# Attention with pooled keys and a routed MLP on one core: even blocks of batches 0 to 2 turn one key tile on TensorE instead of two

## The chip, the core and the metric

The kernel runs on one core of one Trainium2 chip. The metric is the device time of one execution in microseconds (us); lower is better. A comparison takes the kernel before and the changed kernel in turn on the same chip.

## The reference

For each of four batches there are 12288 queries of 128 channels and a key/value map that is pooled 4x4 to 768 rows and multiplied with `w_sr`; keys and values are the same rows. The attention output then goes through a routed MLP: the 128 rows with the highest gate score are replaced by themselves plus a gated two-layer MLP.

```python
def _attn_ref(q, kv, w_sr):
    kv_pool = kv.reshape(B, H // r, r, W // r, r, C).mean(axis=(2, 4))   # r = 4
    k = v = kv_pool.reshape(B, -1, C) @ w_sr
    s = (q @ k.transpose(0, 2, 1)) / np.sqrt(C)
    a = np.exp(s - s.max(-1, keepdims=True))
    a /= a.sum(-1, keepdims=True) + 1e-09
    return a @ v

def _moe_ref(x, w_gate, w1, w2, capacity):
    scores = np.einsum('bsd,d->bs', x, w_gate)
    for b in range(B):
        top = np.argpartition(-scores[b], capacity)[:capacity]
        ye = np.maximum(x[b, top] @ w1, 0.0) @ w2
        out[b, top] = x[b, top] + sigmoid(scores[b, top])[:, None] * ye
```

## The kernel before

The queries are cut into 192 blocks of 256 (48 a batch). A block has two query tiles of 128, so 2 x 768 = 1536 score columns, that is 12 key tiles of 128x128. One main loop runs over the blocks, `for i in range(nb)`, and its body writes out by hand the order in which each engine gets its instructions; every instruction is chained to the one before it on its engine (`InOrder`, line 54), so nothing is reordered later. All instructions therefore have line 54 in the profile, and one goes by the names of the tiles.

In iteration i: TensorE forms the scores of block i+1 in PSUM (`S`, tile `s`, two buffers of three banks, each score as three matmuls: `kl,qh`, `kb,ql`, `kh,qh`) and multiplies the turned exponentials of block i-5 with the values (`AV`, tile `o_two`, 36 matmuls). VectorE takes the row maxima of block i (`s_max`, tile `m`). ScalarE takes the exponentials of block i (`exp`, tile `am`). These have to be turned (transposed) before they can be multiplied with the values, as an f16 high half and a bf16 low half (`hl` before turning, `at` after it). There are two ways:

- Most tiles go through the DMA queue: `to_high` (a cast on ScalarE) and `to_low` (a subtraction on GpSimd) write the two halves into `hl`, and `turn` issues one DMA transposition for each half from SyncE. `hl` has four buffers, `at` six.
- The last `turned(n)` tiles of the block are turned by TensorE (`turn_pe`, matmul `s<-cst,am`), into the PSUM bank that the exponentials have left free. ScalarE then casts them and VectorE subtracts, straight into `at`.

Where fewer than two tiles are turned by TensorE, `own(n)` is 256: ScalarE leaves 256 columns of exponentials in PSUM (`exp` part 1 in place), casts them from there (`hl<-s`), and VectorE takes their low halves in the next iteration instead of GpSimd. `main(n)` is the number of columns that is left for GpSimd; DMA turns `main(n) + own(n)`. Before the change, blocks of batches 0 to 2 have two tiles turned, own 0 and main 1280, so DMA turns 10 tiles in each half. In batch 3 even blocks have none turned, own 256 and main 1280 (12 tiles by DMA), odd blocks one turned, own 256 and main 1152 (11 tiles).

SyncE issues all plain loads and stores and all transpositions from one queue: in each pair of blocks four transpositions, one load of q (256 KB), one store of the output (256 KB), and, while a batch's successor is prepared (`next_keys`, batches 0 to 2), quarter loads of kv (256 KB). GpSimd also adds up the kv rows for the pooling (`kv_sum`) and takes the low halves of the queries (`ql`, every second block). Every few blocks TensorE projects a pooled key tile, and from the second batch on a selection of the 128 rows of the batch before (`topk`, `pick`) runs beside the blocks.

Of the kernel before, what the change touches and what calls it, by code (L numbers as in the profile page):

```python
# [30 lines left out]
NBLK = N // BLK  # L31
# [37 lines left out]
def attention_topk_mlp(ctx, tc, a, outs, capacity):  # L69
# [343 lines left out]
    def direct(n):  # L413
        return n >= nb - 2

    def turned(n):
        return 2 if n < 3 * NBLK else 0 if direct(n) else n % 2

    def own(n):
        return OWN if turned(n) < 2 and not direct(n) else 0  # L420

    def main(n):
        return 2 * M - turned(n) * P - own(n)
# [25 lines left out]
    def turn_pe(n):  # L449
        st[n]["bank2"] = []  # L450
        for c in range(turned(n)):
            lo = 2 * M - (turned(n) - c) * P
            r = pe.transpose(s_flat[n % 2][:, lo:lo + P], st[n]["a"][:, main(n) + c * P:main(n) + (c + 1) * P], ident)
            others(r, [st[n]["exp1"]])
            st[n]["bank2"].append(r.ins)
# [436 lines left out]
    n = nb - 1  # L892
# [154 lines left out]
```

## Time and profile before

| | |
|---|---|
| median of 3 runs | 930.14 us (926.39 to 936.0) |
| profiled execution | 928.83 us, its span 927.1 us |
| TensorE (PE) busy | 891.5 us, 96% |
| ScalarE (ACT) busy | 756.4 us, 82% |
| GpSimd (POOL) busy | 737.7 us, 80% |
| VectorE (DVE) busy | 700.3 us, 76% |
| mean granted TensorE clock | 0.991 |
| DMA moved | 209.82 MB, mean 226 GB/s |

The engines' shares are means over the whole span. Matmuls are pipelined, so a matmul's own duration overlaps that of its neighbours; the pace of TensorE is read from the distance between the starts of things that happen once in a block. A DMA share is the time that packets took, over 16 engines; packets overlap, so it can exceed 1. SPq is the issuing queue of SyncE.

### The profile page before, as it was taken

The page shows a single profiled execution, that of the slowest core. Times are in us where ns is not written, and L with a number is a line of the kernel's source. Part 1 is how long each engine was busy: PE and PEld are TensorE (multiplying, and loading weights), DVE is VectorE, ACT ScalarE, POOL GpSimd, SP SyncE. Part 2 cuts the span into 40 slices and gives each one's busy share as a digit, 9 for nine tenths or more (in the row PEclk, how much of TensorE's full clock was granted, in tenths as well). Part 3 has the DMA queues.
Part 4 walks back from the last instruction along what each step waited for, and adds up shares of the span by engine and source line. Part 5 has one row for each costly group of instructions (what it writes and reads, how often), then busy time and mean ns, then how long its engine had stood idle before and what let it go on. Part 6 is the DMA issues. An engine that isn't in the chain of part 4 may idle for free.

```text
span 927.1 us, 26215 instructions
## 1 busy us (share of the span) xinstructions
PE 891.5 (96%) x10151; PEld 722.3 (78%) x10151; DVE 700.3 (76%) x1861; ACT 756.4 (82%) x1238; POOL 737.7 (80%) x511
## 2 busy tenths in 40 slices
PE   4899999999999999999999999999999999999966
PEld 4678887887788878787787888887788787878865
DVE  6667666767678877777767887888767888888874
ACT  2788888888988888888988888888898988898841
POOL 2788988998898989888888898898787777777711
PEclk9999999999999999999999999999999999999978
DMA  9999999999999999999999999999999999999960
GB/s 363 204 197 237 237 235 244 227 236 245 205 228 236 225 238 235 235 237 217 235 242 230 234 239 229 237 240 219 232 225 225 240 241 231 231 243 231 221 126 21
DMA packets 563517, 209.82 MB, mean 226 GB/s; under 512 B 527040, under 2 KB 528576, under 8 KB 563008
## 3 DMA queue, kind: packets, MB, share of 16 engines
q1 hardware_dynamic: 563136, 207.62, 111.1%
q8 instruction: 79, 1.29, 0.6%
q0 software_dynamic: 256, 0.52, 0.2%
q14 instruction: 46, 0.38, 0.1%
HBM read 52.04 MB, written 25.43 MB: 84 GB/s over the span
## 4 chain that ended last, share of the span: by engine, by line
PE 76%; POOL 9%; issue 6%; DMA 4%; DVE 3%; ACT 2%; SPq 0%; POOLq 0%; DVEq 0%; ACTq 0%
PE s L54 41%; PE o_two L54 34%; POOL hl L54 3%; POOL kv_sum L54 3%; DMA at<-hl 3%; POOL ql L54 2%; DMA kv_raw<-in_kv 1%; ACT am L54 1%; DVE junk L54 1%; PE lot L54 1%; ACT hl L54 0%; DVE m L54 0%; DMA xe<-out,idx 0%; SPq L54 0%; DVE pooled L54 0%
## 5 line engine op out<-in xcount | busy, mean ns | idle before, releaser
L54 POOL TENSOR_TENSOR hl<-am,hl 128x1280 bf16<-128x1280 f32 x192 | 499.3, 2600 | 130.9 <-ACT hl L54 65.0
L54 PEld LDWEIGHTS <-at 128*128 128x128 f16 (+1 forms) x6912 | 399.7, 97 | 54.3 <-issue 51.4
L54 PE MATMUL o_two<-vx,at 128*128 128x130 f16 x6768 | 430.3, 220 | 2.6 <-POOL vx L54 1.5
L54 ACT ACTIVATE am<-s,m 128x512 f32<-128x512 f32 (+1 forms) x528 | 358.3, 706 | 37.6 <-DVE m L54 26.5
L54 DVE TENSOR_REDUCE m<-s 128x2 f32<-128x1536 f32 x191 | 335.5, 1757 | 48.8 <-PE s L54 48.8
L54 PE MATMUL s<-kh,qh 128*128 128x256 f32 (+1 forms) x771 | 362.3, 472 | 0.0
L54 PE MATMUL s<-kl,qh 128*128 128x256 bf16 (+1 forms) x771 | 255.2, 331 | 1.1 <-DVE pm L54 0.9
L54 PE MATMUL s<-kb,ql 128*128 128x256 bf16 (+1 forms) x771 | 250.5, 325 | 1.7 <-POOL ql L54 0.6
L54 ACT CAST hl<-am 128x1280 f16<-128x1280 f32 x192 | 240.4, 1252 | 8.6 <-DMA at<-hl 2.7
L54 PEld LDWEIGHTS s<-kh,qh 128*128 128x128 f32 x771 | 146.3, 190 | 47.6
L54 DVE TENSOR_TENSOR at<-s,at 128x256 bf16<-128x256 f32 (+1 forms) x167 | 67.7, 406 | 91.7 <-ACT at L54 91.7
L54 POOL TENSOR_TENSOR ql<-q_raw,qh 128x512 bf16<-128x512 f32 x96 | 122.5, 1276 | 11.7 <-ACT qh L54 11.7
L54 PEld LDWEIGHTS <-qh 128*128 128x128 bf16 x771 | 75.0, 97 | 58.6 <-issue 49.2
L54 ACT CAST at<-s 128x256 f16<-128x256 f32 (+1 forms) x167 | 59.7, 357 | 67.5 <-PE s L54 67.4
L54 PEld LDWEIGHTS <-ql 128*128 128x128 bf16 x771 | 76.1, 99 | 8.9 <-POOL ql L54 5.7
L54 DVE TENSOR_TENSOR x<-o_two,rz 128x256 f32<-128x256 f32 x186 | 77.4, 416 | 0.0
L54 DVE TENSOR_SCALAR rz<-o_two,sg 128x2 f32<-128x2 f32 x187 | 40.6, 217 | 33.4 <-PE o_two L54 32.5
L54 PE MATMUL s<-cst,am 128*128 128x128 f32 x311 | 62.1, 275 | 2.2 <-ACT am L54 2.1
L54 ACT CAST qh<-q_raw 128x512 fp32r<-128x512 f32 x96 | 59.5, 619 | 3.8 <-DMA q_raw<-in_q 3.8
L54 POOL TENSOR_TENSOR kv_sum<-kv_raw 128x256 f32<-128x256 f32 x72 | 52.7, 732 | 0.0
L54 PEld LDWEIGHTS s<-cst,am 128*128 128x128 f32 x311 | 36.4, 140 | 4.8 <-ACT am L54 3.8
L54 DVE RECIPROCAL rz<-rz 128x2 f32<-128x2 f32 x190 | 31.6, 166 | 6.5
(209 smaller groups left out, 545.5 us busy)
## 6 DMA issues: line engine op xcount, KB each, us to landing
out<-x SPq DMA_DIRECT2D x94, 256.0 KB, 4.1
q_raw<-in_q SPq DMA_DIRECT2D x93, 256.0 KB, 3.3
kv_raw<-in_kv SPq DMA_DIRECT2D x70, 256.0 KB, 4.1
at<-hl SPq DMA_TRANSPOSE x384, 4.1
kv_raw<-in_kv SPq DMA_DIRECT2D x3, 1024.0 KB
kv_raw<-in_kv SPq DMA_DIRECT2D x5, 512.0 KB, 10.2
q_raw<-in_kv SPq DMA_DIRECT2D x2, 512.0 KB
w<-in_w SPq DMA_DIRECT2D x2, 512.0 KB, 8.3
```

Source lines behind the costliest of these rows:

```text
L54: r = f(*args, **kwargs)
```

## The change

`turned(n)` gives 1 in even and 2 in odd blocks of batches 0 to 2, where it gave 2 in all. `own` and `main` follow from it by the unchanged lines under it: even blocks then have own 256 and main 1152.

```diff
     def turned(n):
-        return 2 if n < 3 * NBLK else 0 if direct(n) else n % 2
+        return 1 + n % 2 if n < 3 * NBLK else 0 if direct(n) else n % 2
 
     def own(n):
         return OWN if turned(n) < 2 and not direct(n) else 0
 
     def main(n):
         return 2 * M - turned(n) * P - own(n)
```

TensorE, in an even block of batch 0, the difference (s_113 and s_114 are the two score buffers, `cst` holds the identity):

```order
 L54 MATMUL s_114<-kh,qh 128x256
 L54 MATMUL s_113<-cst,am 128x128 [waits Activation_49]
-L54 MATMUL s_113<-cst,am 128x128
 L54 LDWEIGHTS qh
 L54 MATMUL s_114<-kl,qh 128x256
```

One of the two turning matmuls is gone; nothing else moves on TensorE there.

SyncE, a stretch of batch 1, before:

```order
L54 DMA out<-x 128x512
L54 DMA_TRANSPOSE at<-hl 128x10x128 x2
L54 DMA q_raw<-in_q 128x512
L54 DMA_TRANSPOSE at<-hl 128x10x128
L54 DMA kv_raw<-in_kv 128x512
L54 DMA_TRANSPOSE at<-hl 128x10x128
L54 DMA out<-x 128x512
```

and the same stretch after the change:

```order
L54 DMA out<-x 128x512
L54 DMA_TRANSPOSE at<-hl 128x11x128 x2
L54 DMA q_raw<-in_q 128x512
L54 DMA_TRANSPOSE at<-hl 128x10x128
L54 DMA kv_raw<-in_kv 128x512
L54 DMA_TRANSPOSE at<-hl 128x10x128
L54 DMA out<-x 128x512
```

The order is the same; both transpositions of an even block carry 11 tiles instead of 10.

VectorE, an odd block of batch 1 during a selection (`up`, `tl`, `junk`), from its row maxima to those of the next block, before:

```order
L54 TENSOR_REDUCE m<-s_114 128x2
L54 TENSOR_SCALAR up<-s_113 128x1
L54 TENSOR_SCALAR tl<-up,tl 128x1
L54 TENSOR_SCALAR junk,cnt<-lot,tl 128x96
L54 TENSOR_SCALAR rz<-o_two,sg 128x2
L54 RECIPROCAL rz<-rz 128x2
L54 TENSOR_TENSOR sc<-o_two,rz 128x2
L54 TENSOR_TENSOR x<-o_two,rz 128x256
L54 TENSOR_TENSOR at<-s_114,at 128x256
L54 TENSOR_REDUCE m<-s_113 128x2
```

and after the change:

```order
L54 TENSOR_REDUCE m<-s_114 128x2
L54 TENSOR_TENSOR hl<-s_113,hl 128x256
L54 TENSOR_SCALAR up<-s_113 128x1
L54 TENSOR_SCALAR tl<-up,tl 128x1
L54 TENSOR_SCALAR junk,cnt<-lot,tl 128x96
L54 TENSOR_SCALAR rz<-o_two,sg 128x2
L54 RECIPROCAL rz<-rz 128x2
L54 TENSOR_TENSOR sc<-o_two,rz 128x2
L54 TENSOR_TENSOR x<-o_two,rz 128x256
L54 TENSOR_TENSOR at<-s_114,at 128x256
L54 TENSOR_REDUCE m<-s_113 128x2
```

The even block's share of low halves (`hl<-s_113,hl`) has come in behind the odd block's row maxima; in the even block itself (not shown) `at<-s_113,at` has 128 columns instead of 256.

## Rows read from the trace of the kernel before

**Rows 1.** The page: DMA share in 40 slices; the chain by line.

```profile
DMA  9999999999999999999999999999999999999960
...
PE s L54 41%; PE o_two L54 34%; POOL hl L54 3%; POOL kv_sum L54 3%; DMA at<-hl 3%; POOL ql L54 2%; DMA kv_raw<-in_kv 1%; ACT am L54 1%; DVE junk L54 1%; PE lot L54 1%; ACT hl L54 0%; DVE m L54 0%; DMA xe<-out,idx 0%; SPq L54 0%; DVE pooled L54 0%
```

**Rows 2.** Busy time by stretch; at the end PE clock, DMA share, GB/s.

```profile
280.00:500.00 220.00, 217.28 (x2473) 175.09 (x2472) 167.56 (x443) 184.71 (x295) 190.93 (x131) 1.00 1.17 233
720.00:880.00 160.00, 159.97 (x1903) 128.76 (x1901) 136.91 (x385) 142.06 (x235) 118.58 (x78) 1.00 1.20 233
```

**Rows 3.** Timeline of VectorE: start us, us, instruction, idle before and its releaser.

```profile
404.25 1.76 DVE L54 TENSOR_REDUCE m<-s 128x2 f32<-128x1536 f32 x1 [0.19 <-PE s L54]
...
407.99 0.42 DVE L54 TENSOR_TENSOR at<-s,at 128x256 bf16<-128x256 f32 x1 [0.44 <-ACT at L54]
408.61 1.76 DVE L54 TENSOR_REDUCE m<-s 128x2 f32<-128x1536 f32 x1 [0.19 <-PE s L54]
...
762.02 1.76 DVE L54 TENSOR_REDUCE m<-s 128x2 f32<-128x1536 f32 x1 [0.43 <-PE s L54]
...
766.17 1.76 DVE L54 TENSOR_REDUCE m<-s 128x2 f32<-128x1536 f32 x1 [0.54 <-PE s L54]
...
770.42 1.76 DVE L54 TENSOR_REDUCE m<-s 128x2 f32<-128x1536 f32 x1 [0.43 <-PE s L54]
```

**Rows 4.** Timeline of SyncE's DMA queue.

```profile
387.95 4.01 SPq L54 DMA_TRANSPOSE at<-hl  x2
392.01 0.57 SPq L54 DMA_DIRECT2D q_raw<-in_q  x1
```

**Rows 5.** Up to 325.1: count, ns min/median/max, first and last start.

```profile
L54 SPq DMA_TRANSPOSE at<-hl x129: 1257/1437/3913, 29.7 to 325.0; - x129
L54 ACT CAST hl<-am x67: 1257/1259/1259, 28.4 to 322.3; 128x1280 f16<-128x1280 f32 x67
```

**Rows 6.** The same up to 709.

```profile
L54 SPq DMA_TRANSPOSE at<-hl x301: 1257/1447/3913, 29.7 to 709.0; - x151
L54 ACT CAST hl<-am x151: 1173/1259/1272, 28.4 to 707.4; 128x1280 f16<-128x1280 f32 x148, 128x1152 f16<-128x1152 f32 x3
```

**Rows 7.** The same up to 229.4, 407, 624.1, 665.3 and 848.9.

```profile
L54 SPq DMA_TRANSPOSE at<-hl x89: 1257/1462/3214, 29.7 to 229.4; - x89
L54 ACT CAST hl<-am x46: 1257/1259/1259, 28.4 to 229.3; 128x1280 f16<-128x1280 f32 x46
...
L54 SPq DMA_TRANSPOSE at<-hl x165: 1257/1441/3913, 29.7 to 406.9; - x165
...
L54 SPq DMA_TRANSPOSE at<-hl x261: 1257/1460/3913, 29.7 to 624.0; - x131
L54 ACT CAST hl<-am x132: 1257/1259/1261, 28.4 to 619.4; 128x1280 f16<-128x1280 f32 x132
...
L54 SPq DMA_TRANSPOSE at<-hl x281: 1257/1447/3913, 29.7 to 665.2; - x141
...
L54 SPq DMA_TRANSPOSE at<-hl x365: 1257/1461/3913, 29.7 to 848.9; - x183
```

**Rows 8.** Timeline of ScalarE.

```profile
391.12 1.26 ACT L54 CAST hl<-am 128x1280 f16<-128x1280 f32 x1 [1.01 <-DMA at<-hl]
```

**Rows 9.** Groups by form: busy us, mean ns, idle before and releaser.

```profile
L54 POOL TENSOR_TENSOR hl<-am,hl 128x1280 bf16<-128x1280 f32 x167 | 438.3, 2624 | 87.8 <-ACT hl L54 49.4 <-PE s L54 12.0 <-POOL kv_sum L54 9.5
...
L54 DVE TENSOR_TENSOR at<-s,at 128x256 bf16<-128x256 f32 x144 | 61.2, 425 | 89.1 <-ACT at L54 89.1
...
L54 DVE TENSOR_TENSOR hl<-s,hl 128x256 bf16<-128x256 f32 x46 | 19.1, 415 | 0.0
...
L54 DVE TENSOR_TENSOR at<-s,at 128x128 bf16<-128x128 f32 x23 | 6.5, 284 | 2.5 <-ACT at L54 2.5
```

**Rows 10.** DMA transpositions from 60 to 235 and from 720 to 860.

```profile
L54 SPq DMA_TRANSPOSE at<-hl x79: 1257/1471/3214, 59.2 to 234.8; - x79
...
L54 SPq DMA_TRANSPOSE at<-hl x66: 1289/1468/3457, 718.7 to 859.7; - x66
```

## The prediction

> **What bounds the kernel now.** I read the page's busy shares, chain and DMA slices first, then the timeline block by block, then the counts of one queue against the engines that feed it. The busy shares name TensorE, and the chain of work that ended last agrees: 41% and 34% of it are the scores and the product with the values, 3% a wait for a DMA transposition [rows 1]. The DMA slices say something else as well: the DMA engines stand at nine tenths in every slice but the last two [rows 1], and the share in the middle batches is 1.17, in batch 3 1.20 [rows 2].
>
> TensorE's pace is seen between two row-maximum reductions on VectorE, which start when a block's scores are complete. Batch 1, two turned tiles: 404.25 to 408.61, a block of 4.36 us. Batch 3: a block with none takes 762.02 to 766.17, 4.15 us, and one with a single tile 766.17 to 770.42, 4.25 us [rows 3]. These three repeat to the hundredth wherever nothing disturbs, so a turned tile costs TensorE 0.10 to 0.11 us.
>
> The second pace is that of the DMA queue on SyncE. It issues without a pause: two transpositions from 387.95 for 4.01 us, and at 392.01 the next load [rows 4]. To see whether it keeps up, count transpositions against the casts that feed them (two transpositions per block). At 325.0 the 129th starts, the first of the 65th block; 67 casts have begun by then, the last at 322.3 [rows 5]. The 65th began two blocks of 4.36 us earlier, at about 313.6, and took 1.26 us, so this transposition stood in the queue for 10 us. At 709.0 the 301st starts; its cast, the 151st, began at 707.4 [rows 6]: 0.3 us of waiting. At 229.4 one block waits (89 transpositions, 46 casts, the last just begun) [rows 7]. So the queue falls behind while a batch loads the next batch's kv, and catches up where there is none. Ten us is about all it can fall behind: the casts write one of four buffers, and at 391.12 ScalarE had stood 1.01 us for a buffer whose transposition had not landed [rows 8]. In batch 1 TensorE already runs at the queue's pace, though the page shows it as busy.
>
> The queue's own pace per pair of blocks (four transpositions, one load of q, one store): with kv loads, the 89th to the 165th transposition in 406.9 - 229.4 = 177.5 us, 9.34 us a pair; without them, the 261st to the 281st in 41.2 us, 8.24 a pair; in batch 3, the 301st to the 365th in 139.9 us, 8.74 a pair [rows 6, 7]. TensorE wants 8.72 and in batch 3 8.40 (plus what projections and selections add). **The queue is slower than TensorE in batches 0 and 1 and most of 2, and again in batch 3, and is never dry between the first blocks and 709 us.**
>
> **The change part by part.** It alters the 72 even blocks of batches 0 to 2.
>
> TensorE: one of two turning matmuls goes: 72 x 0.11 = 7.9 us at most [rows 3]. Its first score part on the middle bank now also waits for VectorE's share of the block before; in batch 3, where that wait stands in every block, blocks run at 4.15 and 4.25, so it costs nothing there.
>
> GpSimd: the low halves shrink from 1280 to 1152 columns, a tenth of 2624 ns [rows 9], some 0.25 us less. It doesn't end later than it did, so nothing waits for it; what it hands over earlier joins the queue. Nothing gained.
>
> ScalarE: the cast of turned tiles halves, the big cast loses a tenth, one cast of 128x256 is added. Its bound is the odd blocks of batch 3, which have just this set and run at 4.25. Taken as nothing; its cover is the wait for TensorE's turning.
>
> VectorE: in the even block the turned part falls from 425 to 284 ns; in the following odd block 415 ns come between reduction and sums [rows 9], while that block keeps its 425. There is 0.44 us of waiting in that block, ahead of the turned part [rows 3], so the 415 ns fit, with 0.03 us to spare during a selection. Taken as nothing, bound below.
>
> SyncE: as many issues in the same order, but in even blocks both transpositions carry 11 tiles instead of 10: **two more tiles a pair**. This is the term that decides, and no row shows 11 tiles beside kv loads. From below: batch 3 carries 46 tiles a pair against 40 in the stretch without kv, 8.74 - 8.24 = 0.50 us for six, 0.083 us each. From above: a tile is 128x128 of 2 bytes, 32.8 KB, and the queue moves 233 GB/s [rows 2], 0.141 us each. I take 0.115, the middle. Below both: the medians of a transposition's issue are 1471 ns with 10 tiles and 1468 with 11 or 12 [rows 10], which would make a tile free on SyncE itself; that is a rival.
>
> The Vector page of the Trainium skill ("VectorE: DVE Perf Modes", section "The three transpose paths") speaks against the change: it gives a 128x128 tile 390 ns on TensorE and 1309 ns by DMA, and its rules send such a tile to TensorE where PSUM will do. Taken as a price that would be 144 x 1.309 = 188 us, an estimate from that page; the rows above show neither figure as a pace, about 0.11 us on TensorE and 0.08 to 0.14 in the queue, but the order of the two may hold.
>
> **The sum.** Blocks 4 to 142 hold 70 even blocks: 70 x 2 x 0.115 = 16.1 us more work for a queue that has no gap before 709.0. Its 301st transposition moves to about 725. TensorE may be ahead of it by up to 10 us, where it was 0.3 us ahead; how much of that is left at that point follows from the stretch before. From 624.0 to 709.0 the lead fell from 7.7 us (at 624.0 the 131st block is served; the 132nd cast had begun at 619.4, so the 131st ended near 616.3) to 0.3, so by 7.4 us [rows 6, 7]. Seven changed pairs lie there, each 0.23 us dearer to the queue and 0.11 us shorter on TensorE: 7.4 - 7 x 0.34 = 5.0. It enters at the limit of 10, so some 5.0 us are left. TensorE's delay at 709 is then 16.1 - (5.0 - 0.3) = 11.4 us. In batch 3 the queue falls behind by 8.74 - 8.40 = 0.34 us in each of some 17 pairs, 5.8 us; from 5.0 that passes the limit by 0.8. Together 12.2 us. The profiled execution was 928.83 us (its span 927.1 and 1.7 around it), 1.3 us under the median 930.14: 928.8 + 12.2 = **941.0**. With 0.083 a tile: 11.6 us of work, 4.5 left, 7.4 + 0.3 = 7.7, or 936.5. With 0.141: 19.7, 5.3 left, 14.7 + 1.1 = 15.8, or 944.6. With the looseness of the limit, 935 to 947 for this case.
>
> **The rivals.** *The queue has room (not slower).* Its back-to-back issue would be stretched by easy waiting and shrink when pressed. Then TensorE's 7.9 us count in full: 928.8 - 7.9 = 920.9, and the few us of waits as at 391.12 don't grow. For it: TensorE is the chain, and issue takes 1.26 us at its shortest and 1.47 in the middle [rows 10]. Against it: 9.34 a pair for 177 us with up to 10 us of ready work waiting. The Trainium skill ("DMA: Bandwidth & Descriptors", section "Where 436 GB/s comes from") takes this side: transposition within SBUF is bound by the fabric at 435 GB/s, so a queue that moves less would have room. This trace shows 233 GB/s [rows 2] from a queue that does not keep up, which speaks against it. Chance 0.13. It decides from the point where a pair with kv needs less than 8.61 us of the queue.
>
> *The queue is full, but a tile is cheap.* At 0.04 us a tile: 5.6 us of work, 7.4 - 7 x 0.19 = 6.1 drained, 3.9 left, +2.0, or 931. With a free tile the lead at 709 alone changes, some 2 to 3 us less, 926. So 926 to 935. For it the equal medians [rows 10]; against it the 0.50 us of batch 3. Chance 0.22.
>
> *A tile is dearer beside kv loads*, since loads and transpositions disturb each other: from 0.16 us on, 947 to 953. Chance 0.07.
>
> *VectorE becomes the bound of odd blocks.* If the 415 ns miss their gap by 0.2 us in each, 72 x 0.2 = 14.4 less the 7.9: 935. Against it: batch 3 carries 415 + 284 ns in blocks of 4.25, and its gap before the reduction is still 0.43 [rows 3]. Chance 0.04.
>
> That the change would not do what it says is excluded by the order: 11 tiles, one turning matmul.
>
> **How the numbers follow.** The forecast's case has 0.54. One per cent of the median, about what a measurement of this kernel can tell from no change, is 9.3 us: slower begins at 939.4, faster ends at 920.8. Of the forecast's 0.54 about 0.39 lie above 939.4, with the dear tile 0.46 slower. Of the room case 0.11 lie below 920.8. The rest, 0.43, is within. The range 922 to 949 leaves out the room case and most of the dear tile, under 0.2.
>
> **What would show it.** In the profile after: even blocks of 4.25 us near 80 us, where the queue isn't yet at its limit; then in batches 0 and 1 blocks stretched by ScalarE, TensorE and GpSimd standing for landed transpositions, the share of DMA transpositions in the chain far over 3%; pairs with kv at 9.5 to 9.6 us; 10 us of lead reached before the end of batch 0, and several us of it left near block 150. It is wrong if undisturbed blocks of 4.25 and 4.36 alternate through batch 1, or if a pair with kv still takes 9.3 us.

## The result, and the profile of the changed kernel

The changed kernel takes 940.82 us (median of 4 runs, 938.45 to 944.18), the kernel before 930.2 us (median of 4, 926.39 to 936.0). The ratio is 1.0114, with an interval of 1.0084 to 1.0144. It is slower by 10.6 us; the forecast was 941.0. The profiled execution is the slowest of the four, 944.18 us with a span of 942.3, so its trace shows some 3 us more loss than the median. That forecast and median lie 0.2 us apart is luck: the forecast was a shift of 12.2 us, laid on an execution 1.3 us under its median, and the medians are 10.6 apart.

The page of the changed kernel: busy time of each engine; clock and DMA share in 40 slices; the chain by engine and by line.

```profile
PE 891.0 (95%) x10079; PEld 716.1 (76%) x10079; DVE 714.5 (76%) x1933; ACT 757.9 (80%) x1310; POOL 720.0 (76%) x511
...
PEclk9999999999999999999999999999999999999968
DMA  9899999999999999999999999999999999999950
...
PE 58%; DMA 17%; POOL 9%; issue 6%; DVE 5%; ACT 3%; SPq 1%; POOLq 0%; ACTq 0%; DVEq 0%
PE s L54 31%; PE o_two L54 27%; DMA at<-hl 15%; POOL hl L54 4%; POOL ql L54 2%; POOL kv_sum L54 2%; DVE m L54 2%; ACT am L54 1%; ACT hl L54 1%; DMA kv_raw<-in_kv 1%; SPq L54 1%; DVE junk L54 1%; PE lot L54 1%; ACT at L54 0%; DVE rz L54 0%
```

The busy shares and the DMA slices look like those of before; they don't tell of any loss. The chain does: the wait for a DMA transposition went from 3% [rows 1] to 15%, and TensorE's two entries fell from 75% to 58%.

Busy time by stretch (columns as in [rows 2]):

```profile
280.00:500.00 220.00, 212.94 (x2424) 170.29 (x2422) 171.36 (x465) 183.22 (x314) 183.07 (x130) 1.00 1.18 235
720.00:880.00 160.00, 159.67 (x1874) 127.30 (x1871) 135.19 (x386) 142.13 (x233) 120.56 (x80) 1.00 1.21 233
```

In the 220 us of the first stretch TensorE does 2424 matmuls instead of 2473 [rows 2]. Of the 49 that are missing, 26 are turning matmuls, which the change takes away (73 instead of 99 read `cst`); the other 23, about a quarter of what a pair needs, it did not get to. With less to do in each pair it did not do more pairs but slightly fewer, so it stands there. The queue moves 235 GB/s where it moved 233, hardly more than before.

VectorE's timeline, the starts of row maxima early in batch 0, then a pair of blocks in batch 1:

```profile
69.15 1.76 DVE L54 TENSOR_REDUCE m<-s 128x2 f32<-128x1536 f32 x1 [0.19 <-PE s L54]
73.37 1.76 DVE L54 TENSOR_REDUCE m<-s 128x2 f32<-128x1536 f32 x1 [0.43 <-PE s L54]
77.70 1.76 DVE L54 TENSOR_REDUCE m<-s 128x2 f32<-128x1536 f32 x1 [0.19 <-PE s L54]
...
290.60 1.76 DVE L54 TENSOR_REDUCE m<-s 128x2 f32<-128x1536 f32 x1 [0.43 <-PE s L54]
292.28 0.41 DVE L54 TENSOR_TENSOR hl<-s,hl 128x256 bf16<-128x256 f32 x1
...
293.81 0.42 DVE L54 TENSOR_TENSOR x<-o_two,rz 128x256 f32<-128x256 f32 x1
294.34 0.42 DVE L54 TENSOR_TENSOR at<-s,at 128x256 bf16<-128x256 f32 x1
294.96 1.76 DVE L54 TENSOR_REDUCE m<-s 128x2 f32<-128x1536 f32 x1 [0.19 <-PE s L54]
...
299.20 1.76 DVE L54 TENSOR_REDUCE m<-s 128x2 f32<-128x1536 f32 x1 [0.43 <-PE s L54]
```

Where nothing disturbs, an even block takes 4.22 to 4.24 us (69.15 to 73.37, 294.96 to 299.20) and an odd one 4.33 to 4.36 (73.37 to 77.70, 290.60 to 294.96), as forecast. In the odd block VectorE's new 0.41 us at 292.28 fits, during a selection: the turned part at 294.34 no longer waits, and the next reduction starts when the scores are there, as before.

The queue's own counts, up to 237.9, 722.9 and 863.9 us (columns as in [rows 5]):

```profile
L54 SPq DMA_TRANSPOSE at<-hl x89: 1258/1497/3617, 30.1 to 237.8; - x89
L54 ACT CAST hl<-am x47: 1155/1175/1259, 28.9 to 235.8; 128x1152 f16<-128x1152 f32 x24, 128x1280 f16<-128x1280 f32 x23
...
L54 SPq DMA_TRANSPOSE at<-hl x301: 1257/1506/3617, 30.1 to 722.8; - x151
L54 ACT CAST hl<-am x151: 1154/1258/1272, 28.9 to 719.5; 128x1280 f16<-128x1280 f32 x76, 128x1152 f16<-128x1152 f32 x75
...
L54 SPq DMA_TRANSPOSE at<-hl x365: 1257/1504/3617, 30.1 to 863.8; - x183
```

At 237.8 the 45th block's first transposition is issued, and the 47th block's cast has begun: the queue is two blocks behind in batch 0 already, where in the kernel before it was one block behind at the same transposition (229.4 [rows 7]). At block 151 the cast starts 12.1 us later than before (719.5 against 707.4 [rows 6]), and its transposition 13.8 us later (722.8 against 709.0).

Who waits for a landed transposition (engine, tile, waited for: us in total, times, longest), in the kernel before

```profile
POOL hl L54 <- DMA at<-hl: 3.6, 3, 1.8
ACT hl L54 <- DMA at<-hl: 2.7, 5, 1.0
PEld L54 <- DMA at<-hl: 2.0, 5, 0.6
```

and in the changed one:

```profile
ACT hl L54 <- DMA at<-hl: 33.8, 35, 3.3
PEld L54 <- DMA at<-hl: 23.9, 34, 2.1
PE o_two L54 <- DMA at<-hl: 14.1, 25, 1.5
```

One such wait on ScalarE, in its timeline:

```profile
353.39 0.91 ACT L54 ACTIVATE am<-s,m 128x768 f32<-128x768 f32 x1
357.59 0.37 ACT L54 CAST hl<-s 128x256 f16<-128x256 f32 x1 [3.30 <-DMA at<-hl]
```

The cast needs one of the four `hl` buffers, and the transposition that reads it has not landed. TensorE in the same block:

```profile
355.70 0.85 PE L54 MATMUL o_two<-vx,at 128*128 128x130 f16 x12 [1.50 <-DMA at<-hl]
357.56 0.52 PE L54 MATMUL o_two<-vx,at 128*128 128x130 f16 x6 [1.01 <-DMA at<-hl]
```

It stands for `at` tiles: the engines at both ends of the queue wait for it. ScalarE's wait was there before, with 1.01 us [rows 8].

### The profile page after: what moved, and what is told of

Same layout as the page of the kernel before. It is cut to its first block, busy times and chain, and to the rows that moved or that the text cites. A ratio compares the mean times of both kernels' runs of the same rounds, so it can differ in the third digit from the quotient of the medians.

```text
span 942.3 us, 26302 instructions
## 1 busy us (share of the span) xinstructions
PE 891.0 (95%) x10079; PEld 716.1 (76%) x10079; DVE 714.5 (76%) x1933; ACT 757.9 (80%) x1310; POOL 720.0 (76%) x511
## 4 chain that ended last, share of the span: by engine, by line
PE 58%; DMA 17%; POOL 9%; issue 6%; DVE 5%; ACT 3%; SPq 1%; POOLq 0%; ACTq 0%; DVEq 0%
PE s L54 31%; PE o_two L54 27%; DMA at<-hl 15%; POOL hl L54 4%; POOL ql L54 2%; POOL kv_sum L54 2%; DVE m L54 2%; ACT am L54 1%; ACT hl L54 1%; DMA kv_raw<-in_kv 1%; SPq L54 1%; DVE junk L54 1%; PE lot L54 1%; ACT at L54 0%; DVE rz L54 0%
## 5 line engine op out<-in xcount | busy, mean ns | idle before, releaser
L54 POOL TENSOR_TENSOR hl<-am,hl 128x1152 bf16<-128x1152 f32 (+1 forms) x192 | 481.8, 2510 | 160.6 <-ACT hl L54 105.5
L54 PE MATMUL o_two<-vx,at 128*128 128x130 f16 x6768 | 434.8, 220 | 16.1 <-DMA at<-hl 14.1
L54 ACT ACTIVATE am<-s,m 128x512 f32<-128x512 f32 (+2 forms) x456 | 332.5, 746 | 31.5 <-DVE m L54 28.8
L54 ACT CAST hl<-am 128x1152 f16<-128x1152 f32 (+1 forms) x192 | 233.8, 1218 | 15.0 <-DMA at<-hl 11.6
L54 DVE TENSOR_TENSOR at<-s,at 128x128 bf16<-128x128 f32 (+1 forms) x167 | 58.0, 348 | 71.1 <-ACT at L54 69.4
L54 ACT CAST at<-s 128x128 f16<-128x128 f32 (+1 forms) x167 | 52.0, 311 | 52.6 <-PE s L54 51.4
L54 ACT CAST hl<-s 128x256 f16<-128x256 f32 x118 | 43.8, 371 | 22.3 <-DMA at<-hl 22.2
L54 PE MATMUL s<-cst,am 128*128 128x128 f32 x239 | 54.5, 277 | 1.9 <-ACT am L54 1.9
L54 ACT ACTIVATE s<-s,m 128x256 f32<-128x256 f32 x118 | 52.9, 448 | 3.8
```

The lines of the kernel that those rows point to most:

```text
L54: r = f(*args, **kwargs)
```

## The experiments

Ratios are against the kernel before unless said otherwise, with 95% intervals. "Changed kernel" is the one with the change. Where microseconds are worked out from a ratio, the base is 930.2.

**The change without its tiles.**

```diff
+        k = QT * KT - turned(n) - int(n < 3 * NBLK and n % 2 == 0)
+        return sp.dma_start_transpose(out=st[n]["at"][:, h, 0:k], in_=st[n]["hl"][:, h, 0:k * P])
...
+            kw = 3 if j and kt == 4 and n < 3 * NBLK and n % 2 == 0 else kt
```

> The changed kernel, with every engine's instructions as they are, but in even blocks of batches 0 to 2 both DMA transpositions carry 10 tiles and not 11 (the eleventh tile is left out, and its place in the product is taken by a neighbour's). If the DMA queue's two extra tiles a pair are the whole loss, TensorE's shorter blocks show: 928.8 - 7.9 - some 2 us of old waits, about 919, a ratio to the kernel before of 0.988 to 0.992. If VectorE's and ScalarE's added share in the odd and even blocks is what costs, nothing of that is taken away and it stays at 1.005 to 1.014.

Measured: 929.8 us, 0.9962 [0.9927, 0.9996]. The loss is gone, so it lies in the two tiles and not in TensorE's, VectorE's or ScalarE's new shares. But only 3.5 us of TensorE's 7.9 came out, less than I expected. The waits tell why:

```profile
ACT hl L54 <- DMA at<-hl: 19.2, 21, 2.0
PEld L54 <- DMA at<-hl: 11.6, 17, 1.5
PE o_two L54 <- DMA at<-hl: 7.9, 14, 1.3
```

Even with 10 tiles the queue does not follow a faster TensorE all the way. The prediction had said so ("with a free tile the lead at 709 alone changes", 926); my expectation had dropped it.

**The tiles without the change.** The kernel before, with an eleventh tile that nobody reads in both transpositions of even blocks. GpSimd clears its columns, 0.32 us a pair more on that engine.

```diff
+        k = QT * KT - turned(n) + more_tiles(n)
+        return sp.dma_start_transpose(out=st[n]["at"][:, h, 0:k], in_=st[n]["hl"][:, h, 0:main(n) + own(n) + more_tiles(n) * P])
```

> The kernel before with two turned tiles in every block, but in even blocks of batches 0 to 2 both DMA transpositions carry an eleventh tile that nobody reads (GpSimd clears its columns first). If the queue is the bound: 16 us more work, of which the lead takes in 4 to 5: 939 to 942, a ratio of 1.009 to 1.014, as if the whole change were there. If the loss comes from the engines' new shares or from the order: 1.000 to 1.003.

Measured: 942.11 us, 1.0112 [1.0053, 1.0172], as large as the whole loss. The waits for transpositions rise in the same places (ScalarE 19.8 us in 25, TensorE's weight loads 11.0 in 18); the chain shows some of it through GpSimd (`POOL hl`, 12% against 3% [rows 1]), whose clearing writes `hl` too:

```profile
PE s L54 27%; PE o_two L54 23%; POOL hl L54 12%; DMA at<-hl 9%; POOL kv_sum L54 4%; POOL ql L54 4%; ACT hl L54 1%; DMA kv_raw<-in_kv 1%; DVE junk L54 1%; ACT am L54 1%; SPq L54 1%; PE lot L54 1%; DVE m L54 0%; DMA xe<-out,idx 0%; POOL kv_proj L54 0%
```

The clearing is 72 x 0.32 = 23 us of work on GpSimd that the changed kernel does not have, and this run does not part it from the tiles. That the tiles cost rests on the run before and the next one, which add nothing to any engine.

**Two tiles fewer than before.**

```diff
+        k = QT * KT - turned(n) - int(n < 3 * NBLK and n % 2 == 0)
+        return sp.dma_start_transpose(out=st[n]["at"][:, h, 0:k], in_=st[n]["hl"][:, h, 0:k * P])
```

> The kernel before, but in even blocks of batches 0 to 2 both DMA transpositions carry 9 tiles instead of 10 (one tile is left out, a neighbour stands in for it in the product). TensorE's work is unchanged. If the kernel before is bound by TensorE except for the few blocks where the queue's lead is used up, this takes those 2 to 3 us away: ratio 0.996 to 0.999, and hardly any wait for a landed transposition is left. If the kernel before already runs at the queue's pace through batches 0 to 2: 16 us less queue work, ratio 0.983 to 0.990.

Measured: 926.41 us, 0.9942 [0.9913, 0.997], between the two and nearer to the first. Hardly a wait for a landed transposition is left (GpSimd 3.3 us, TensorE's weight loads 0.8). So some 5.4 us of the kernel before (2.8 to 8.1 by the interval) were the queue's, and what is left at 926 is, by the chain, TensorE's. A tile more in even blocks is thus worth about 10.4 us upwards, clearing included, and a tile less 5.4 downwards: the kernel before stands near the point where queue and TensorE are equally slow.

**Half the bytes of q, as many DMAs.**

```diff
-            load_q(nb_, nblk // BPC, nblk % BPC * BLK, (nblk % BPC + 2) * BLK)
+            load_q(nb_, nblk // BPC, nblk % BPC * BLK, (nblk % BPC + (1 if nb_ < 3 else 2)) * BLK)
...
+        if b < 3:
+            raw = raw[:, 0:1].broadcast_to([P, 2, BLK])
```

> The changed kernel, but each load of q in the main loop of batches 0 to 2 moves 256 columns instead of 512 (131 KB less, as many DMAs), and the second block of a pair takes the queries of the first, so the output differs. A pair's queue work loses as many bytes as four tiles of a transposition hold. If the queue's time goes with bytes, this takes away about 4 x 0.1 = 0.4 us a pair, twice what the change added: TensorE sets the pace, 921 to 929 us, 0.977 to 0.988 of the changed kernel. If it goes with the number of DMAs and with the tiles of transpositions, not with the bytes of a plain load, nothing changes: 0.997 to 1.003.

Measured: 921.87 us, 0.9871 [0.9813, 0.9929], some 0.976 of the changed kernel (0.9871 / 1.0114). Relieved of 131 KB a pair, the change does make the kernel faster, as the first rival had it: by 12.0 us, of which the 5.4 that nine tiles took away are one part. The other 6.6 would be TensorE's 7.9, but the two ratios leave it uncertain by some 6 us.

```profile
POOL hl L54 <- DMA at<-hl: 4.1, 4, 1.8
ACT hl L54 <- DMA at<-hl: 2.2, 4, 0.9
```

**Is it SyncE's issuing, or the moving?** Three kernels give DMAs to ScalarE's queue, so that SyncE issues fewer. First the changed kernel and the kernel before with the loads of q moved:

```diff
-        sp.dma_start(out=qraw[b, ch][:, lo:hi], in_=a["q"][:, b, ch, lo:hi])
+        issue.dma_start(out=qraw[b, ch][:, lo:hi], in_=a["q"][:, b, ch, lo:hi])
...
+            load_q(nb_, nblk // BPC, nblk % BPC * BLK, (nblk % BPC + 2) * BLK, act)
```

> The changed kernel with the loads of q issued by ScalarE instead of SyncE; the same transfers, one issue fewer a pair on SyncE. The 512-byte issues cost some 0.3 us each, near their own time on SyncE, so I now hold the issuing on SyncE for the limit. Then 0.57 + 0.1 us a pair come off the queue, more than the eleventh tiles put on it, and TensorE's shorter blocks show: ratio to the kernel before 0.987 to 0.994. If moving the data is the limit, whoever issues it, nothing changes: 1.007 to 1.014. If the issue holds ScalarE up for its 0.57 us and ScalarE can't hide that, it is slower than both, 1.015 or more.

> The kernel before with the loads of q issued by ScalarE. If the issuing on SyncE is the limit, this does what nine tiles did: 0.993 to 0.997. If moving the data is the limit: 0.999 to 1.002. If ScalarE can't hide the issue: above 1.003.

Measured: 946.45 us, 1.014 [1.0071, 1.0208], and 933.5 us, 1.0017 [0.9983, 1.0052]. The time gains nothing, but the queue does. In the kernel before with q by ScalarE:

```profile
L54 SPq DMA_TRANSPOSE at<-hl x165: 1252/1590/3801, 30.1 to 398.9; - x165
L54 ACT CAST hl<-am x84: 1257/1259/1260, 28.8 to 398.4; 128x1280 f16<-128x1280 f32 x84
```

The 165th transposition starts at 398.9 us instead of 406.9 [rows 7], and the queue is one block behind where it was two (84 casts begun instead of 85). In the changed kernel with q by ScalarE, few waits of ScalarE for a landed transposition are left:

```profile
ACT hl L54 <- DMA at<-hl: 4.4, 5, 2.1
```

In their place it stands before its own issue, as here in its timeline:

```profile
403.03 1.16 ACT L54 CAST hl<-am 128x1152 f16<-128x1152 f32 x1
406.34 0.34 ACTq L54 DMA_DIRECT2D q_raw<-in_q  x1
406.77 0.69 ACT L54 ACTIVATE am<-s,m 128x512 f32<-128x512 f32 x1 [2.59 <-POOL hl L54]
```

Between 50 and 710 us ScalarE stands for over 1 us around 12 of its 70 loads, 29 us in all, and TensorE's weight loads for the scores wait 25.7 us for its exponentials, against 3.5 in the changed kernel. That is the third case of the expectation, so this run does not decide between issuing and moving. With the kernel before only 2 of 73 loads hold ScalarE that long; why the relieved queue gave no time back there stays open.

The transpositions between 60 and 700 us of the changed kernel (count, then ns min/median/max of the issue), as it is and with q by ScalarE:

```profile
L54 SPq DMA_TRANSPOSE at<-hl x277: 1257/1522/3617, 59.4 to 697.6; - x139
```

```profile
L54 SPq DMA_TRANSPOSE at<-hl x275: 1252/1693/4993, 58.7 to 697.7; - x138
```

With a load of q less in each pair on SyncE, its transpositions take longer to issue. In both traces each starts only after its cast has ended, so the longer issue is no wait for ScalarE's data: the time of an issue on this queue is not fixed, and a share of SyncE's busy time does not say how much of it could be saved. The Trainium skill ("DMA: Bandwidth & Descriptors", section "Issuing engines are not separate DMA queues") says that DMAs of all issuing engines run on the same 16 DMA engines and interleave, and that a second issuer saves the initiating alone. That neither run is faster fits this, with ScalarE's own standing in both times.

Then one tile turned in all blocks of batches 0 to 2, with q and the output by ScalarE:

```diff
-        return 1 + n % 2 if n < 3 * NBLK else 0 if direct(n) else n % 2
+        return 1 if n < 3 * NBLK else 0 if direct(n) else n % 2
...
+            return (act if n < 3 * NBLK else sp).dma_start(out=outs[b].rearrange("(h p j) d -> h p j d", p=P, j=JPC)[ch, :, h * QT:(h + 2) * QT], in_=x[:, k:k + 2 * QT])
```

> One turned tile in all blocks of batches 0 to 2 (11 tiles by DMA in every block), with the loads of q and the stores of those batches issued by ScalarE. If the issuing on SyncE is the limit: 2 x 0.67 us a pair off the queue, 4 x 0.1 on it, and TensorE shorter by 0.22 a pair, 16 us in all with 2 to 3 of old waits on top: ratio 0.980 to 0.987. If moving the data is the limit: the loss of the change twice over, 1.02 to 1.03.

Measured: 981.32 us, 1.0539 [1.0455, 1.0623], beyond both. ScalarE waits 59.7 us in 28 times for transpositions; it issues DMAs itself here, and stands for over 1 us around 30 of 134 of them (50 to 710 us), 70 us in all. So this run does not decide either.

**A DMA with hardly any bytes.** One of 512 bytes in every block of batches 0 to 2, added to the kernel before.

```diff
+        if 0 < i < 3 * NBLK:
+            sp.dma_start(out=nib.tile([1, P], F32, name="nib"), in_=a["cst"][0:1, 0:P])
```

> The kernel before with one more DMA per block of batches 0 to 2 on SyncE's queue, of 512 bytes only. If the queue's limit is the issuing on SyncE (0.57 us and a gap of 0.1 for a plain DMA), two a pair make 1.3 us, a pair with kv takes 10.7 us instead of 9.3, and the kernel takes 85 us more, about 1015, a ratio of 1.09. If the limit is the moving of the data by the DMA engines, the extra issues fit beside it: 930 to 940, a ratio of 1.00 to 1.01.

Measured: 969.08 us, 1.0378 [1.0319, 1.0437]. Neither theory: 143 of them cost some 35 us, a quarter of a microsecond each (0.21 to 0.28 by the interval). SyncE's timeline shows them at 0.28 and 0.44 us:

```profile
405.74 0.57 SPq L54 DMA_DIRECT2D q_raw<-in_q  x1
406.36 0.28 SPq L54 DMA_DIRECT2D nib<-in_cst  x1
406.75 1.85 SPq L54 DMA_TRANSPOSE at<-hl  x1
408.64 0.58 SPq L54 DMA_DIRECT2D kv_raw<-in_kv  x1
409.33 2.60 SPq L54 DMA_TRANSPOSE at<-hl  x1
411.98 0.44 SPq L54 DMA_DIRECT2D nib<-in_cst  x1
```

**One DMA more or fewer for the same bytes.** In the changed kernel, each store of batches 0 to 2 in two halves:

```diff
+                sp.dma_start(out=o_[ch, :, h * QT:(h + 1) * QT], in_=x[:, k:k + QT])
+                return sp.dma_start(out=o_[ch, :, (h + 1) * QT:(h + 2) * QT], in_=x[:, k + QT:k + 2 * QT])
```

> The changed kernel, but each store of the output in batches 0 to 2 goes as two DMAs of half the columns: the same bytes, one DMA more a pair. If the queue's time goes with bytes, nothing changes: 0.997 to 1.004 of the changed kernel. If each DMA costs about 0.3 us by itself, as the 512-byte DMAs did, 70 pairs lose 20 us, less the pairs in which the queue has room: 1.012 to 1.024.

Measured: 962.5 us, 1.0302 [1.0238, 1.0366], about 1.019 of the changed kernel: some 17 us for 72 DMAs more, 0.24 us each (0.15 to 0.33 by the intervals), as a cost for each DMA would have it. That suggested merging, which changes no result and could have beaten both kernels:

```diff
-        if i % 2 and i - 1 + BPC < nb:
+        if i % 4 == 1 and i - 1 + BPC < nb:
...
-            load_q(nb_, nblk // BPC, nblk % BPC * BLK, (nblk % BPC + 2) * BLK)
+            load_q(nb_, nblk // BPC, nblk % BPC * BLK, (nblk % BPC + 4) * BLK)
...
+            w = 4 if n < nb - 12 else 2
```

> The changed kernel, with one load of q for four blocks (512 KB) and one store of the output for four blocks (512 KB, up to 12 blocks from the end), so one DMA less a pair and the same bytes. If a DMA costs about 0.3 us of the queue beside its bytes, this gives back more than the 0.2 us a pair that the change added, TensorE sets the pace, and the time is 921 to 930 us: 0.990 to 0.999 of the kernel before. If the fixed cost belongs to small or split DMAs alone, the time stays at that of the changed kernel: 1.009 to 1.014 of the kernel before.

> The kernel before, with the same merged loads and stores. Its queue has then about 0.3 us a pair to spare and TensorE alone sets the pace: only the few stalls can go, as with nine tiles, 0.992 to 0.998 of the kernel before, and the changed kernel with merged transfers should stand 2 to 6 us under it (TensorE's 7.9 us less the stalls that are left). If transfers of 512 KB hold up the transpositions behind them, it is not faster: 0.999 to 1.006.

Measured: 946.4 us, 1.0153 [1.0115, 1.0191], and 937.55 us, 1.0055 [1.0028, 1.0082]. Fewer DMAs give nothing back; the kernel before loses by them. SyncE's timeline of the latter:

```profile
403.15 1.34 SPq L54 DMA_TRANSPOSE at<-hl  x1
404.54 0.57 SPq L54 DMA_DIRECT2D kv_raw<-in_kv  x1
405.21 11.43 SPq L54 DMA_TRANSPOSE at<-hl  x5
```

Five transpositions in a row take 11.43 us, 2.29 each. But one by one they take 4.34, 1.62, 1.44, 1.32 and 1.93 us: it is the first, behind the loads, that is long, and one of 3.91 us stands at 310.91 in the kernel before too. A small DMA costs 0.24 us where it is added, and is not worth that where it is taken away. The expectation named one reason, that transfers of 512 KB hold up the transpositions behind them. It fits that a transposition lands 4.6 us after its issue (median) in both merged kernels and 4.1 in the two others, but that this is the cause isn't shown.

**The change in batch 1 alone**, because the pace there had not risen (next section).

```diff
-        return 2 if n < 3 * NBLK else 0 if direct(n) else n % 2
+        return 1 + (n % 2 or n // NBLK != 1) if n < 3 * NBLK else 0 if direct(n) else n % 2
```

> The change in the 24 even blocks of batch 1 alone; batches 0 and 2 as before. If every pair with two more tiles costs the queue about 0.2 us, the stretch from the 89th to the 165th transposition takes 9.45 to 9.6 us a pair, against 9.34 before, the 24 pairs cost 5 us of queue work, and the whole 2 to 6 us: 1.002 to 1.006 of the kernel before. If the queue's pace in batch 1 doesn't go with its tiles, as the 9.30 us in the changed kernel suggest, the stretch stays at 9.2 to 9.35 us a pair and the whole within 0.998 to 1.002.

Measured: 935.63 us, 1.002 [0.9992, 1.0047], which both theories allow. Its stretch from the 89th to the 165th transposition took 9.39 us a pair, between the two as well. But the trace shows what such a stretch is worth:

```profile
L54 SPq DMA_TRANSPOSE at<-hl x87: 1257/1452/4950, 29.5 to 230.4; - x87
L54 ACT CAST hl<-am x46: 1258/1259/1259, 28.2 to 230.1; 128x1280 f16<-128x1280 f32 x46
```

Batch 0 is here the kernel before, unchanged. Yet by 230.4 this queue has issued 87 transpositions, where that of the kernel before had issued 89 by 229.4 [rows 7], so it is two blocks behind its casts and not one; it had lost 0.3 us a pair in batch 0 (9.45 from the 17th to the 69th transposition, 9.14 in the other trace). One trace cannot tell 0.2 us a pair.

## Why the prediction was right, step by step

**The queue, not TensorE, sets the end: right.** Taking the tiles away removes the loss, the tiles alone (with their clearing) make as much, and with fewer bytes in the queue the same change is 12 us faster than the kernel before. What limits the queue itself, issues or bytes, stays open: both added DMAs of no size and removed bytes moved the time. Of the rivals, "the queue has room" is out with the result and became true only when the loads of q were halved. "A tile is cheap" (926 to 935) and "a tile is dearer" (from 947 on) lie outside the 938.45 to 944.18 of the runs. One sign was read too strongly: that the queue "issues without a pause". Between 230 and 700 us its issues fill 93% of the time in the kernel before, and 91% with nine tiles, where TensorE sets the pace. It is the count against the casts that told of the backlog.

**TensorE's 7.9 us: right by the block.** Undisturbed even blocks are 4.22 to 4.24 us, 0.11 to 0.12 under the odd ones. As a whole it is not measured: the 6.6 us that the change gains beyond the queue's 5.4, once the queue is relieved, could be off by as much.

**GpSimd, ScalarE, VectorE at nothing: right** for all that shows: the two runs that keep these edits and relieve the queue are faster, and VectorE's 0.41 us fit in the odd block.

**Two tiles a pair at 0.115 us: of the right size.** The changed kernel against the same one without its tiles is 1.0114 / 0.9962 = 1.0153, some 14 us for 144 tiles or 0.10 us a tile, 0.07 to 0.13 by the two intervals. That lies within the bounds of 0.083 and 0.141 and says no more. Single traces don't narrow it. The 301st transposition moved by 13.8 us, not 16.1: 13.8 / 140 = 0.099 us a tile. With the tiles alone it stood at 720.8, 11.8 / 140 = 0.084. But with the change in batch 1 alone, 48 tiles, it stood at 718.7, which would be 0.20. The median issue rose from 1447 ns [rows 6] to 1506.

**The lead left at block 150, 5.0 us: too much.** The cast there started at 719.5 and took 1.3 us; its transposition was issued at 722.8, so some 2 us were left. In this trace a smaller queue shift and a smaller lead offset each other, which is luck: the shift of TensorE was 12.1 us where 11.4 was forecast. Both sizes rest on single traces, which by the last experiment scatter as much as they are off by. Whole against whole, the forecast's shift was 12.2 us, the medians give 10.6 and the two profiled executions 15.2.

**Batch 3, +0.8: right in sign.** The 365th transposition is 14.9 us late (863.8 against 848.9 [rows 7]), 1.1 more than the 301st. The tail adds a little in this execution, the slowest of the four: 942.3 - 927.1 = 15.2.

**"Pairs with kv at 9.5 to 9.6 us": wrong as a sign.** The 17th to the 69th took 9.51 a pair, but the 89th to the 165th (237.8 to 414.6) took 9.30, and 9.18 with the tiles alone, where the kernel before took 9.34 [rows 7]. I had written that the prediction is wrong if a pair with kv still takes 9.3. In batch 1 it did, and the loss came all the same. The sign was badly chosen: such a pace scatters by 0.3 us between traces of the same program. What did show it, as named, are the stretched blocks, the waits for landed transpositions (the rows above add up to 8 us before and 72 after) and the chain, 3 to 15%. The sum of such waits is a sign and no measure of the loss: without the tiles it was still 39 us, at 0.9962, and with q by ScalarE some 11 us, at 1.014.

## What to carry to other kernels

Where an engine and a queue are equally slow, taking work from the one and giving it to the other loses on the side that gets it: compare what has been issued with what has been made ready, block by block, before trusting the busy share of the engine. The time of an issue is not fixed, so its length does not tell what taking an issue away gives: here taking bytes away gave time back, and merging DMAs or giving them to another engine did not. An engine that takes over issues can stand for them itself, so look at its waits too. Between two traces of one execution each, differences of 3% in the pace of a stretch mean nothing here; the ratio of the medians has to carry the verdict.

## What the runs showed of the hardware that was not expected

- A DMA of 512 bytes on this loaded queue cost about 0.25 us of the whole (35 us for 143), and splitting a 256 KB store in two cost 0.24 us, though halving the number of q loads and stores gained nothing.
- The issue of a transposition stretched when ScalarE took over the loads of q: from a median of 1522 to 1693 ns in the changed kernel and from 1462 to 1572 in the kernel before (60 to 700 us). The DMA moved 225 to 229 GB/s over the span in the changed kernel, with split stores and with merged transfers alike.
- A load of q that ScalarE issues held it for over 1 us in 12 of 70 cases in the changed kernel, up to 3.9 us.
